# A list of moves behind a list scheduler: 97 operations change places on their engines

## Chip, cores and metric

The kernel runs on one core of a Trainium2 chip. The metric is the device time of one execution in microseconds (us), the median of three runs. A core has a matmul engine (TensorE, PE in the profile; its weight loads are PEld), VectorE (DVE), ScalarE (ACT), GpSimd (POOL), and SyncE (SP), which here only issues DMAs.

## What is computed

Three layers follow one another. Attention over 2 batches, 8 heads, 768 positions of 64 numbers, where each position sees the first 8 positions and its last 96:

```python
scores = scale * np.matmul(q, k.transpose(0, 1, 3, 2)) + bias       # bias: slope of the head times the distance
scores = np.where(is_global | is_local, scores, -1000000000.0)
a = np.exp(scores - max); a = a / (sum + 1e-09)
x = np.matmul(a, v)                                                 # heads put side by side: (2, 768, 512)
```

Then a layer that mixes each position with the one before it, and a normalised feed-forward layer:

```python
xk = mu_k * x + (1.0 - mu_k) * x_prev
xr = mu_r * x + (1.0 - mu_r) * x_prev
x = 1.0 / (1.0 + np.exp(-(xr @ w_r))) * (np.maximum(xk @ w_k, 0.0) ** 2 @ w_v)
xn = (x - mu) / np.sqrt(var + 1e-06) * g_ln
return x + np.maximum(xn @ w_ch1, 0.0) @ w_ch2                      # w_ch1: 512 x 2048
```

The weights arrive as words of 64 bits and are made into 32-bit numbers on the chip.

## The kernel before

**Stages.** The attention goes by 12 blocks of 128 positions. For each, queries and keys are loaded (`plan_loads`), turned by TensorE (`plan_turn`, L443), multiplied to scores (`plan_scores`, L496), given the bias and their minimum by VectorE (`least`, L509), exponentiated by ScalarE (`exp`, L515), turned (L546) and multiplied with the values (`values` in `plan_weighted`, L561). `plan_out` scales and turns the result: GpSimd adds a small constant to the sums (L587), VectorE takes the reciprocal (L588), GpSimd spreads it over a tile (L591), TensorE turns it (four instructions, L598), ScalarE copies it back, and VectorE multiplies. Every 256 positions are a group of the mixing layer (`plan_mix`, L699 to L711; its products L755 and L791). In the last layer both products are done by a scheme of seven half-size products with each operand split in a high and a low part (L1089, L1190 to L1192).

**Weights.** `plan_words` makes a piece of 128 x 512 weights: a DMA into a tile (L625), a copy of the high words with a factor by ScalarE (L343) or GpSimd (L347), and three integer steps of VectorE (L628, L629, L630). `split` then makes the high part (ScalarE, L636) and the low part (L640). The third and fourth piece of w_r have a tile of their own, `s1`; the others take turns in two tiles `stage`.

**Array forms.** Scores have operands of 64 rows (the code calls this "rows"), value products have 64 output columns ("columns"), and all others use the whole array. One value product of a block and four heads is 8 or 16 instructions in the trace, one score product 8.

**Order.** Every function registers operations with `Plan.op`: the engines that may do it with an estimated time, the cells read and written, the tiles, and a due time. There are 2222. `Plan.play` then builds the order: of the operations whose inputs are done and whose tiles are free it takes the one that can start first by its estimates, then the one due first, gives it to an engine and issues it. A change of form is counted with 95 ns (`SWITCH`). Each engine runs its instructions in the order of issue and waits for results of the others; PE, DVE, ACT and POOL keep the order written down. `first` (L911 on) registers the whole program and calls `play`.

Of the kernel before, what the change touches and what calls it, by code (L numbers as in the profile page):

```python
# [43 lines left out]
UP, LEAD = 15.6, 10.0  # L44
WARM = 9
FILL = {0: 4, 1: 3, 2: 3, 3: 2}
SCALE = 0.125
BIG = 2.0**38
SM_EPS = 1e-9
# [3 lines left out]
def slope(h):  # L53
    return 2.0 ** (-8.0 * (h + 1) / H)
# [56 lines left out]
class Plan:  # L111
# [29 lines left out]
        self.ops.append((engines, fn, deps, rooms, due, size, mode))  # L141
        return i

    def play(self):
        n = len(self.ops)
        wait = [len(x[2]) for x in self.ops]
        users = [[] for _ in self.ops]
        for i, x in enumerate(self.ops):
            for d in x[2]:
                users[d].append(i)  # L150
        ready = [0.0] * n
        by = {}
        free = {}
        live = {}
        open_ = [i for i in range(n) if not wait[i]]
        dma, mode = 0.0, ""
        trace = []
        while open_:
            best = None
            for i in open_:  # L160
                engines, _, _, rooms, due, _, _ = self.ops[i]
                at = ready[i]
                ok = True
                for x in rooms:
                    if x.tile is None:
                        if live.get(x.tag, 0) < x.bufs:
                            f = free.setdefault(x.tag, [0.0] * x.bufs)
                            at = max(at, f[0])
                        else:
                            ok = False  # L170
                if not ok:
                    continue
                for e, ns in engines.items():
                    t = max(at, self.clock[e])
                    if len(engines) > 1 and any(max(at, self.clock[g]) + m < t + ns for g, m in engines.items() if g != e):
                        continue
                    key = (t, due, i, e)
                    if best is None or key < best:
                        best = key
            if best is None:  # L180
                raise RuntimeError("no operation can go: " + str([(i, [x.tag for x in self.ops[i][3] if x.tile is None]) for i in open_][:20]))
            t, _, i, e = best
            engines, fn, _, rooms, _, size, way = self.ops[i]
            for x in rooms:
                if x.tile is None:
                    live[x.tag] = live.get(x.tag, 0) + 1
                    free[x.tag].pop(0)
                    x.tile = x.make()
            self.now = t
            fn(e)  # L190
            end = t + engines[e]
            if e == "PE" and way != mode:
                end += self.SWITCH
                mode = way
            self.clock[e] = end - self.OVERLAP.get(e, 0.0)
            if size:
                dma = max(dma, end) + size / 190.0
                end = dma + 1900.0
            trace.append((t, end, e, i))
            for x in rooms:  # L200
                x.left -= 1
                x.end = max(x.end, end)
                if not x.left and not x.hold:
                    live[x.tag] -= 1
                    free[x.tag].append(x.end + self.LAG)
                    free[x.tag].sort()
            open_.remove(i)
            for u in users[i]:
                ready[u] = max(ready[u], end + self.LAG)
                wait[u] -= 1  # L210
                if not wait[u]:
                    open_.append(u)
        assert not any(wait), [i for i in range(n) if wait[i]][:20]
        return trace


class Fast:
# [80 lines left out]
    def query_scale(self):  # L298
        self.qs = self.t([P, 4, 1], "qs")
        for h in range(H):  # L300
            self.nc.gpsimd.memset(self.qs[(h % 2) * D : (h % 2 + 1) * D, h // 2, :], -SCALE / slope(h))

# [172 lines left out]
    def plan_scores(self, i):  # L475
# [25 lines left out]
        op = p.op({"PE": 3.4 * w}, scores, reads, [("S", i)], banks + [self.Q, self.K], due, mode="rows")  # L501
        for x in range(FILL.get(i, 0)):
            self.filler(op, due + 2)
# [407 lines left out]
    def first(self, last):  # L911
# [13 lines left out]
        with self.tc.manual_schedule(engines=ORDERED):  # L925
# [7 lines left out]
            rooms = [self.token("rt", 2), self.token("rt", 2), self.token("e", 2)]  # L933
# [23 lines left out]
            end = self.due(24) + 8  # L957
# [15 lines left out]
            self.plan_second(at[NG])  # L973
            p.op({"DVE": 3000}, lambda e: last(), due=at[NG] + 150, behind=[self.step[8]["P1"]])
            p.op({"PE": 20}, lambda e: self.tc.mark_branch_hint_location("skip", "LikelyTaken", engines=[*ORDERED, mybir.EngineType.SP]), behind=[self.step[8]["P1"]], due=-6.0)
            self.trace = p.play()

    def plan_second(self, start):

# [252 lines left out]
def general_attention(tc, a, w, x_dram, ident):  # L1232

    nc = tc.nc
    with tc.tile_pool(name="ga1", bufs=1) as c1, tc.tile_pool(name="ga2", bufs=2) as c2, \
# [19 lines left out]
        for b in range(B):  # L1255
            for h in range(H):
                t = {}
                for x in "qkv":
                    t[x] = c2.tile([P, NB, D], F32, tag=x, name=x)
                    nc.gpsimd.dma_start(t[x], a[x][b, h].rearrange("(n p) d -> p n d", p=P))  # L1260
                for x, s in (("q", SCALE), ("k", 1.0)):
                    t[x + "T"] = c2.tile([D, S], F32, tag=x + "T", name=x + "T")
# [174 lines left out]
```

## Time and profile before

| what | before |
|---|---|
| median of 3 runs | 535.83 us (535.5 to 535.83) |
| the profiled execution's own time | 535.59 us |
| its span, first to last instruction | 533.8 us |
| TensorE busy | 524.3 us, 3231 matmuls |
| VectorE busy | 411.5 us |
| ScalarE busy | 302.7 us |
| GpSimd busy | 274.7 us |
| DMA | 40.52 MB, 76 GB/s in the mean |

Attention and mixing overlap up to some 130 us; from there to 268 us the mixing layer's last products run, and the seven-product scheme from 268 us to the end. An instruction's row in a timeline has its start, its length and in brackets the idle time of its engine before it with what ended that. Neighbouring instructions of one kind are one row with a count (x16). Lengths of matmul rows include the pipeline, so a time per instruction is taken from one row's start to the next row's start.

### The profile page before, as it was taken

What the parts mean: (1) busy time and instruction counts of PE and PEld (TensorE: products, weight loads), DVE (VectorE), ACT (ScalarE), POOL (GpSimd) and SP (SyncE); (2) the same over time, 40 slices, a digit from 0 to 9 for tenths busy, and PEclk for the clock granted to TensorE, in tenths of its full rate; (3) what the DMA queues carried; (4) which work ended last, traced back from release to release, by engine and by line L of the source; (5) the groups of instructions that cost most, each with busy time, mean ns of one, the idle gap of its engine ahead of it and who ended that gap; (6) DMA issues with size and microseconds to landing.
All of it is one profiled execution on the core that took longest, in us unless ns stands there. A gap on an engine that the chain in (4) does not pass through costs nothing.

```text
span 533.8 us, 8958 instructions
## 1 busy us (share of the span) xinstructions
PE 524.3 (98%) x3231; PEld 457.1 (86%) x3231; DVE 411.5 (77%) x817; ACT 302.7 (57%) x660; POOL 274.7 (51%) x346
## 2 busy tenths in 40 slices
PE   8999999999999999999999999999999999999997
PEld 6877787879899888889887898889998898989885
DVE  5899988965997437559889687778799878878564
ACT  3899998886454135474667454654555545365320
POOL 2487866846753121242238463773865758487300
PEclk9999999999999999999999999999999999999999
DMA  7996474301220000022022003122130312311024
GB/s 160 247 230 184 135 198 121 96 24 26 93 80 2 0 2 1 0 80 80 0 80 79 1 6 115 39 80 80 41 118 1 118 41 61 98 41 39 1 79 160
DMA packets 52110, 40.52 MB, mean 76 GB/s; under 512 B 40928, under 2 KB 41184, under 8 KB 52064
## 3 DMA queue, kind: packets, MB, share of 16 engines
q1 hardware_dynamic: 51200, 39.01, 25.9%
q10 hardware_dynamic: 864, 0.92, 0.5%
q8 instruction: 26, 0.43, 0.3%
q14 instruction: 20, 0.16, 0.1%
HBM read 36.77 MB, written 3.15 MB: 75 GB/s over the span
## 4 chain that ended last, share of the span: by engine, by line
PE 86%; DVE 5%; ACT 4%; POOL 2%; issue 1%; DMA 1%; SPq 0%; ACTq 0%; DVEq 0%
PE b L1089 20%; PE b L791 13%; PE b L1190 8%; PE b L1192 8%; PE b L1191 8%; PE b L755 5%; PE b L828 4%; PE b L830 4%; PE b L829 4%; PE b L561 3%; PE b L496 3%; PE b L546 3%; PE b L443 1%; PE b L527 1%; ACT t0l L515 1%
## 5 line engine op out<-in xcount | busy, mean ns | idle before, releaser
L630 DVE SCALAR_TENSOR_TENSOR cv<-cv,stage 128x512 int32<-128x512 int32 x50 | 45.2, 906 | 2.1 <-DVE stage L629 0.5
L515 ACT ACTIVATE t0l<-t0l,mn 128x232 f32<-128x232 f32 (+1 forms) x96 | 44.3, 467 | 4.3 <-DVE mn L509 4.3
L629 DVE SCALAR_TENSOR_TENSOR stage<-stage 128x512 int32<-128x512 int32 x50 | 46.0, 919 | 0.7
L699 POOL TENSOR_SCALAR rt<-xg,vec 128x256 f32<-128x256 f32 x48 | 31.4, 667 | 19.7 <-DVE m L806 8.6
L1206 DVE TENSOR_TENSOR xg<-b,xg 128x512 f32<-128x512 f32 (+1 forms) x51 | 34.3, 674 | 8.0 <-PE b L1192 6.7
L1108 POOL TENSOR_TENSOR h<-rt,h 128x384 fp32r<-128x384 f32 x28 | 33.4, 1194 | 8.3 <-ACT h L343 8.1
L1108 POOL TENSOR_TENSOR h<-e,h 128x384 fp32r<-128x384 f32 x14 | 15.4, 1103 | 42.7 <-ACT h L343 42.6
L1104 ACT ACTIVATE e<-e 128x384 f32<-128x384 f32 x16 | 8.4, 526 | 48.5 <-DVE e L1097 48.5
L628 DVE TENSOR_SCALAR stage<-stage 128x512 int32<-128x512 int32 x50 | 35.1, 702 | 0.5 <-DMA stage<-in_moe_w_ch_dram 0.5
L704 DVE SCALAR_TENSOR_TENSOR rt<-xg,vec,rt 128x256 f32<-128x256 f32 x48 | 31.0, 691 | 2.4 <-POOL rt L699 2.4
L509 DVE CUSTOM_DVE_ANT_0 t0l<-b,ln 128x232 f32<-128x232 f32 x80 | 27.6, 391 | 5.9 <-PE b L496 5.9
L791 PE MATMUL b<-b0l,t1l 128*128 128x256 f32 x144 | 31.9, 282 | 0.0
L1196 DVE TENSOR_TENSOR xg<-b,xg 128x1024 f32<-128x1024 f32 x23 | 28.0, 1218 | 4.9 <-PE b L1192 4.6
L866 POOL TENSOR_SCALAR st<-st 128x1 f32<-128x1 f32 x12 | 3.8, 315 | 52.4 <-DVE st L863 46.5
L546 PE MATMUL b<-ident,t0l 128*128 128x128 f32 x176 | 28.5, 281 | 0.0
L343 ACT ACTIVATE cv<-stage 128x512 f32<-128x512 f32 x41 | 27.2, 664 | 1.4 <-POOL s L640 0.9
L1089 PE MATMUL b<-t0h,s 128*128 128x384 f32 x128 | 28.0, 340 | 0.0
L1033 ACT ACTIVATE cv<-cv,vec 128x256 f32<-128x256 f32 x32 | 14.6, 502 | 23.5 <-DVE cv L630 23.4
L1089 PE MATMUL b<-t1h,s 128*128 128x384 f32 x128 | 27.6, 337 | 0.0
L640 POOL TENSOR_TENSOR s<-cv,s 128x384 fp32r<-128x384 f32 (+1 forms) x22 | 24.9, 1135 | 4.9 <-ACT s L636 4.9
L755 PE MATMUL b<-s,h 128*128 128x512 f32 x96 | 25.8, 405 | 0.0
L1089 PEld LDWEIGHTS b<-t1h,s 128*128 128x128 f32 x128 | 23.2, 188 | 2.8
(315 smaller groups left out, 1706.0 us busy)
## 6 DMA issues: line engine op xcount, KB each, us to landing
stage<-in_moe_w_ch_dram SPq DMA_DIRECT2D x26, 512.0 KB, 3.9
stage<-in_moe_w_k_dram SPq DMA_DIRECT2D x8, 512.0 KB, 4.5
stage<-in_moe_w_v_dram SPq DMA_DIRECT2D x8, 512.0 KB, 3.6
stage<-in_moe_w_ch_dram SPq DMA_DIRECT2D x12, 256.0 KB, 3.1
b0l<-in_q_dram SPq DMA_DIRECT2D x7, 256.0 KB, 4.5
h<-in_v_dram SPq DMA_DIRECT2D x6, 256.0 KB, 4.3
h<-in_v_dram SPq DMA_DIRECT2D x6, 192.0 KB, 3.1
stage<-in_moe_w_r_dram SPq DMA_DIRECT2D x2, 512.0 KB, 4.7
```

The source lines that it names most:

```text
L515: nc.scalar.activation(t, t, AF.Exp, bias=mn.tile[:, k : k + 1], scale=-1.0, accum_out=sm.tile[:, h : h + 1])
L546: nc.tensor.transpose(b.tile[:, c, k * P : (k + 1) * P], tp.tile[:, o : o + P], self.ident)
L628: p.op({"DVE": 500}, lambda e: nc.vector.tensor_scalar(low(), low(), 29, None, ALU.logical_shift_right), [R], [(R, 1)], [raw], due - 1.3, ...
L629: p.op({"DVE": 760}, lambda e: nc.vector.scalar_tensor_tensor(low(), high(), -(1 << 31), low(), ALU.bitwise_and, ALU.bitwise_or), [R, (R, ...
L630: p.op({"DVE": 760}, lambda e: nc.vector.scalar_tensor_tensor(y(), y(), 3, low(), ALU.logical_shift_left, ALU.bitwise_or), [(R, 2)], [C], ...
L755: nc.tensor.matmul(b.tile, *seq[s], start=s == 0, stop=s == 11)
L791: nc.tensor.matmul(o, l, r, start=s == 0, stop=s == 11)
L1089: nc.tensor.matmul(acc(x), lhs(i, c, n), rhs(r, j, c), start=y == 0, stop=y == 5)
L1108: lambda e: (nc.vector if e == "DVE" else nc.gpsimd).tensor_tensor(o(1), V(y), o(0).bitcast(F32), ALU.subtract),
L1190: nc.tensor.matmul(ps, hi, wh, start=f == 0, stop=False)
L1191: nc.tensor.matmul(ps, hi, wl, start=False, stop=False)
L1192: nc.tensor.matmul(ps, lo, wh, start=False, stop=f == 1)
```

## The change

`play` is cut in three. `choose` finds the order as before. `moved` takes 97 pairs (x, y) and puts operation x just before operation y on the engine that they share; then it merges the queues of the engines again, with the tiles' limits kept. `play` issues the result.

```diff
+MOVES = (
+    (507, 548), (715, 162), (149, 599), (690, 478), (597, 590), (204, 189), (250, 628), (288, 284),
...
-    def play(self):
+    def choose(self):
...
+    def moved(self, chosen):
...
+        for x, y in MOVES:
+            q = lists[home[x]]
+            q.remove(x)
+            q.insert(q.index(y), x)
+            rank[x] = rank[y] - 0.5
...
+            for e, q in lists.items():
+                if place[e] < len(q) and self.ops[q[place[e]]][2] <= done:
+                    i = q[place[e]]
+                    new = {x for x in self.ops[i][3] if x not in made}
+                    if all(live.get(x.tag, 0) + sum(z.tag == x.tag for z in new) <= x.bufs for x in new):
+                        heads.append((rank[i], e, i))
+            _, e, i = min(heads)
...
+    def play(self):
+        for e, i in self.moved(self.choose()):
+            _, fn, _, rooms, _, _, _ = self.ops[i]
+            for x in rooms:
+                if x.tile is None:
+                    x.tile = x.make()
+            fn(e)
```

The instructions are the same ones, and each stays on its engine. 91 different operations are named: 31 of VectorE, 27 of TensorE, 17 of GpSimd, 12 of SyncE, 10 of ScalarE. Counted over the whole queue of TensorE, two neighbouring operations differ in array form 88 times before and 78 times now: value products of one block come together in four places, and score and value products stand side by side in four more. Line numbers of the new file are 58 higher in the functions shown here (L561 is L619).

Four places follow. A row has the line, the operation, the tiles out<-in and the size; a tile's last number only counts tiles, and differs between the files.

SyncE at the start of the program, from the query load of block 2 (b0h<-in_q) on, before; u is the tile of keys, s1 that of the third and fourth piece of w_r:

```order
L402 DMA b0h_15_140<-in_q_dram 128x8x64
L353 DMA h1_1_74<-in_v_dram 96x8x64
L354 DMA h1_1_74<-in_v_dram 32x8x64
L625 DMA stage_16_144<-in_moe_w_r_dram 128x1024
L356 DMA b0h_15_140<-in_k_dram 128x8x64
L625 DMA s1_17_147<-in_moe_w_r_dram 128x1024
L356 DMA h1_1_74<-in_v_dram 128x8x64
L625 DMA s1_17_147<-in_moe_w_r_dram 128x1024
L353 DMA h1_1_74<-in_v_dram 96x8x64
L354 DMA h1_1_74<-in_v_dram 32x8x64
L353 DMA u_13_126<-in_k_dram 96x8x64
L354 DMA u_13_126<-in_k_dram 32x8x64
```

The same place now, from the second block's keys (the first two rows) on; the query load stands ahead of what is shown:

```order
L411 DMA u_13_126<-in_k_dram 96x8x64
L412 DMA u_13_126<-in_k_dram 32x8x64
L411 DMA u_13_126<-in_k_dram 96x8x64
L412 DMA u_13_126<-in_k_dram 32x8x64
L683 DMA s1_20_157<-in_moe_w_r_dram 128x1024
L411 DMA h1_1_74<-in_v_dram 96x8x64
L412 DMA h1_1_74<-in_v_dram 32x8x64
L683 DMA stage_21_161<-in_moe_w_r_dram 128x1024
L414 DMA b0h_15_136<-in_k_dram 128x8x64
L414 DMA h1_1_74<-in_v_dram 128x8x64
L683 DMA s1_20_157<-in_moe_w_r_dram 128x1024
```

The last two rows of before, the fourth block's keys, now stand third and fourth, ahead of both s1 loads.

GpSimd between 19 and 31 us of the profile, before; s1 is the raw tile, cv its copy, sm the softmax sums:

```order
L591 COPY xg_24_178<-sm_29_194 128x4x128
L640 TENSOR_TENSOR s0_39_233<-cv_38_232,s0_39_233 128x512
L425 COPY h1_1_74<-h1_1_74 32x512
L640 TENSOR_TENSOR s0_39_233<-cv_57_329,s0_39_233 128x512
L347 TENSOR_SCALAR cv_66_377<-s1_17_147 128x512
L587 TENSOR_SCALAR sm_53_304<-sm_53_304 128x8
L591 COPY xg_24_178<-sm_53_304 128x4x128
L640 TENSOR_TENSOR s0_39_233<-cv_66_377,s0_39_233 128x512
L347 TENSOR_SCALAR cv_77_437<-s1_17_147 128x512
L425 COPY h1_1_74<-h1_1_74 32x512
```

The same place now:

```order
L649 COPY xg_24_178<-sm_29_194 128x4x128
L698 TENSOR_TENSOR s0_38_231<-cv_37_230,s0_38_231 128x512
L483 COPY h1_1_74<-h1_1_74 32x512
L698 TENSOR_TENSOR s0_38_231<-cv_56_324,s0_38_231 128x512
L405 TENSOR_SCALAR cv_65_372<-s1_20_157 128x512
L405 TENSOR_SCALAR cv_66_374<-s1_20_157 128x512
L645 TENSOR_SCALAR sm_53_304<-sm_53_304 128x8
L649 COPY xg_24_178<-sm_53_304 128x4x128
L698 TENSOR_TENSOR s0_38_231<-cv_66_374,s0_38_231 128x512
L483 COPY h1_1_74<-h1_1_74 32x512
```

The copy from the fourth piece (before: cv_77, now cv_65) has gone from behind the low part L640 to the place ahead of the third piece's copy.

TensorE at 62 to 66 us, before; yy holds the turned exponentials, h1 the values, xg the spread reciprocals that L598 turns:

```order
L546 MATMUL b45_141_875<-ident_60,t0l_18_153 128x128 x6
L561 MATMUL b6_145_902<-yy_41_243,h1_1_74 64x128 x8
L598 MATMUL b3_147_916<-ident_60,xg_135_831 128x128 x4
L561 MATMUL b6_145_902<-yy_41_243,h1_1_74 64x128 x8
L546 MATMUL b45_151_942<-ident_60,t0l_18_153 128x128
L496 MATMUL b2_152_947<-b0h_15_140,b0l_12_123 128x128
```

The same place now:

```order
L604 MATMUL b45_141_875<-ident_60,t0l_16_142 128x128 x6
L656 MATMUL b3_146_906<-ident_60,xg_135_833 128x128 x4
L619 MATMUL b6_148_915<-yy_41_243,h1_1_74 64x128 x16
L604 MATMUL b45_151_942<-ident_60,t0l_16_142 128x128
L554 MATMUL b2_152_947<-b0h_15_136,b0l_12_123 128x128
```

The turns of xg now come first, and the value products of both halves of the block's heads follow in one piece (x16 calls, 32 instructions in the trace).

VectorE at 270 to 273 us, before; L640 makes low parts of weights, L878 subtracts for the normalised input:

```order
L640 TENSOR_TENSOR s1_408_3109<-stage_385_2903,s1_408_3109 128x512
L640 TENSOR_TENSOR s1_408_3109<-cv_398_3028,s1_408_3109 128x384
L640 TENSOR_TENSOR s1_408_3109<-stage_388_2925,s1_408_3109 128x512
L878 TENSOR_TENSOR h1_322_2349<-ln_403_3066,h1_322_2349 128x256 x2
L842 SCALAR_TENSOR_TENSOR xg_415_3160<-e_358_2671,b6_401_3049 128x512
```

The same place now:

```order
L698 TENSOR_TENSOR s1_408_3109<-stage_385_2903,s1_408_3109 128x512
L698 TENSOR_TENSOR s1_408_3109<-cv_398_3028,s1_408_3109 128x384
L936 TENSOR_TENSOR h1_322_2349<-ln_403_3066,h1_322_2349 128x256 x2
L698 TENSOR_TENSOR s1_408_3109<-stage_388_2925,s1_408_3109 128x512
L900 SCALAR_TENSOR_TENSOR xg_415_3160<-e_358_2671,b6_401_3049 128x512
```

The two subtractions L878 now stand ahead of the last of the three L640.

## Rows read from the trace of the kernel before

**Rows 1.** Page of the kernel before: busy time of each engine, granted clock by slice.
```profile
PE 524.3 (98%) x3231; PEld 457.1 (86%) x3231; DVE 411.5 (77%) x817; ACT 302.7 (57%) x660; POOL 274.7 (51%) x346
...
PEclk9999999999999999999999999999999999999999
```

**Rows 2.** Page: the chain that ended last, shares of the span by engine.
```profile
PE 86%; DVE 5%; ACT 4%; POOL 2%; issue 1%; DMA 1%; SPq 0%; ACTq 0%; DVEq 0%
```

**Rows 3.** Windows: us, then busy us (instructions) of each engine, clock, DMA share, GB/s.
```profile
66.00:130.00 64.00, 64.00 (x566) 53.09 (x562) 47.16 (x145) 53.55 (x147) 41.30 (x52) 1.00 0.35 92
...
300.00:500.00 200.00, 200.00 (x996) 179.99 (x995) 160.06 (x233) 103.04 (x203) 124.88 (x138) 1.00 0.19 59
```

**Rows 4.** Chain of waits, 7 to 70 us: start us, us, what the chain goes through.
```profile
26.88 0.39 ACT t0l L515
...
45.07 1.29 POOL h L711
...
57.78 0.72 DVE xg L345
...
62.76 0.80 POOL h L425
```

**Rows 5.** Timeline of TensorE, 42 to 47 and 111 to 120 us: start us, us, instruction.
```profile
44.25 1.97 PE L561 MATMUL b<-yy,h 128*64 128x128 f32 x32
46.15 0.44 PE L546 MATMUL b<-ident,t0l 128*128 128x128 f32 x2
...
116.89 0.60 PE L546 MATMUL b<-ident,t0l 128*128 128x128 f32 x4
117.32 0.60 PE L598 MATMUL b<-ident,xg 128*128 128x128 f32 x4
117.85 1.05 PE L496 MATMUL b<-b0h,b0l 64*128 64x232 f32 x8
```

**Rows 6.** Timeline of TensorE, 63 to 67 us (in brackets idle time, what ended it).
```profile
63.60 1.09 PE L561 MATMUL b<-yy,h 128*64 128x128 f32 x16 [0.57 <-POOL h L425]
64.62 0.66 PE L598 MATMUL b<-ident,xg 128*128 128x128 f32 x4
...
66.24 0.33 PE L546 MATMUL b<-ident,t0l 128*128 128x128 f32 x1
```

**Rows 7.** Timeline of GpSimd, 54 to 68 us.
```profile
58.67 0.80 POOL L591 COPY xg<-sm 128x512 f32<-128x512 f32 x1 [0.20 <-DVE b0h L345]
...
63.50 0.81 POOL L591 COPY xg<-sm 128x512 f32<-128x512 f32 x1
```

**Rows 8.** Timeline of GpSimd, 20 to 34 us.
```profile
23.76 0.86 POOL L347 TENSOR_SCALAR cv<-s 128x512 f32<-128x512 f32 x1
...
28.22 0.84 POOL L347 TENSOR_SCALAR cv<-s 128x512 f32<-128x512 f32 x1
```

**Rows 9.** Timeline of VectorE, 23 to 29 us.
```profile
25.28 0.69 DVE L630 SCALAR_TENSOR_TENSOR cv<-cv,s 128x512 int32<-128x512 int32 x1
...
26.44 0.40 DVE L509 CUSTOM_DVE_ANT_0 t0l<-b,ln 128x232 f32<-128x232 f32 x1 [0.17 <-PE b L496]
```

**Rows 10.** SyncE's timeline; DMAs of 7 to 27 us; loads of tile s, issue to landing.
```profile
14.74 2.65 SPq L625 DMA_DIRECT2D s<-in_moe_w_r_dram  x1
...
DMA packets 12383, 4.69 MB, mean 234 GB/s; under 512 B 11869, under 2 KB 11869, under 8 KB 12381
...
DMA to landing us min/median/max: 6.3/8.0/9.6
```

**Rows 11.** Timeline of VectorE, 266 to 276 us.
```profile
271.44 0.69 DVE L640 TENSOR_TENSOR s<-stage,s 128x512 fp32r<-128x512 f32 x1
272.04 0.88 DVE L878 TENSOR_TENSOR h<-ln,h 128x256 f32<-128x256 f32 x2
...
273.88 0.69 DVE L862 BATCH_NORM_STATS2 st<-xg 128x6 f32<-128x512 f32 x1 [0.36 <-ACT ln L876]
```

**Rows 12.** Timeline of TensorE, 262 to 297 us.
```profile
273.90 0.66 PE L871 MATMUL b<-ident,ln 128*128 128x128 f32 x4 [0.65 <-ACT ln L876]
```

More of the change, by code (lines that the diff above doesn't have):

```diff
@@ L46 @@
 FILL = {0: 4, 1: 3, 2: 3, 3: 2}
+MOVES = (
[13 rows of a table added]
+)
 SCALE = 0.125
@@ L142, in op @@
         return i
-    def play(self):
+    def choose(self):
         n = len(self.ops)
+        left = {x: x.left for o in self.ops for x in o[3]}
+        made = set()
         wait = [len(x[2]) for x in self.ops]
@@ L164, in play @@
                 for x in rooms:
-                    if x.tile is None:
+                    if x not in made:
                         if live.get(x.tag, 0) < x.bufs:
@@ L180, in play @@
             if best is None:
-                raise RuntimeError("no operation can go: " + str([(i, [x.tag for x in self.ops[i][3] if x.tile is None]) for i in open_][:20]))
+                raise RuntimeError("no operation can go: " + str([(i, [x.tag for x in self.ops[i][3] if x not in made]) for i in open_][:20]))
             t, _, i, e = best
-            engines, fn, _, rooms, _, size, way = self.ops[i]
+            engines, _, _, rooms, _, size, way = self.ops[i]
             for x in rooms:
-                if x.tile is None:
+                if x not in made:
                     live[x.tag] = live.get(x.tag, 0) + 1
                     free[x.tag].pop(0)
-                    x.tile = x.make()
-            self.now = t
-            fn(e)
+                    made.add(x)
             end = t + engines[e]
@@ L198, in play @@
                 end = dma + 1900.0
-            trace.append((t, end, e, i))
+            trace.append((e, i))
             for x in rooms:
-                x.left -= 1
+                left[x] -= 1
                 x.end = max(x.end, end)
-                if not x.left and not x.hold:
+                if not left[x] and not x.hold:
                     live[x.tag] -= 1
@@ L214, in play @@
         return trace
+    def moved(self, chosen):
+        rank, home, lists = {}, {}, {}
+        for k, (e, i) in enumerate(chosen):
+            rank[i], home[i] = float(k), e
+            lists.setdefault(e, []).append(i)
+        for x, y in MOVES:
[3 more added lines that the diff above has]
+            rank[x] = rank[y] - 0.5
+        left = {x: x.left for o in self.ops for x in o[3]}
+        place, done, made, live, order = dict.fromkeys(lists, 0), set(), set(), {}, []
+        while len(order) < len(chosen):
+            heads = []
+            for e, q in lists.items():
[5 more added lines that the diff above has]
+            _, e, i = min(heads)
+            place[e] += 1
+            done.add(i)
+            order.append((e, i))
+            for x in self.ops[i][3]:
+                if x not in made:
+                    made.add(x)
+                    live[x.tag] = live.get(x.tag, 0) + 1
+            for x in self.ops[i][3]:
+                left[x] -= 1
+                if not left[x] and not x.hold:
+                    live[x.tag] -= 1
+        return order
+    def play(self):
[5 more added lines that the diff above has]
+            fn(e)
 class Fast:
@@ L975, in first @@
             p.op({"PE": 20}, lambda e: self.tc.mark_branch_hint_location("skip", "LikelyTaken", engines=[*ORDERED, mybir.EngineType.SP]), behind=[self.step[8]["P1"]], due=-6.0)
-            self.trace = p.play()
+            p.play()
     def plan_second(self, start):
```

12 rows, old and new, of the table MOVES are left out of this document.

## The prediction

> **What bounds the kernel now.** I read the share of each engine first [rows 1]: TensorE is busy for 98% of the span and its granted clock is at full speed in every slice, so the clock plays no part. The chain that ended last says the same with an exception [rows 2]: TensorE has 86% of it, the other engines some 11%. Then the stretches [rows 3]: from 66 to 130 us and from 300 to 500 us TensorE has no idle time, so what is taken from its queue there comes off the end, and what other engines do there doesn't count while it stays early enough. In between, two places are set by other engines. The first is 26.5 to 63.6 us [rows 4]: the chain goes through ScalarE's exponentials (26.88), GpSimd (45.07), VectorE (57.78) and GpSimd again (62.76) before TensorE has it back at 63.60. TensorE looks busy there, with short waits, but a delay at the start of the stretch is handed on from one to the next and comes out at its end. The second is 268 to 295 us, where VectorE leads.
>
> My sums are made against the profiled execution, 535.59 us, of which 533.8 are the span and 1.8 lie around it. The median of the three runs is 0.24 higher; a change of 0.2%, about what a measurement of this kernel can tell from none, is 1.07 us. So "same" here means 534.76 to 536.90.
>
> **1. Fewer changes of array form.** No instruction goes or comes; TensorE changes form 78 times in place of 88. Price, from starts to starts: 32 value products in one piece last 1.90 us to the next start (44.25 to 46.15), 16 of them 1.02 (63.60 to 64.62) [rows 5, 6]. Two blocks of 16 apart cost 2.04, so a merge gives 0.14. In addition four turns last 0.53 when another form follows them (117.32 to 117.85) and 0.43 when none does (116.89 to 117.32) [rows 5]: 0.10 for one entry into a form. A merged pair thus saves 0.24, and a score block that comes to stand directly beside a value block saves 0.10. The new order has four merges (the products of the token blocks at 58.5, 63.6, 82.9 and 112.6 us) and four new neighbours (at 24, 70, 89 and 95 us); the merges at 82.9 and 112.6 each lose one neighbourhood they had, so they are worth 0.14. The total is 2 x 0.24 + 2 x 0.14 + 4 x 0.10 = 1.16 us. Only what lies in the TensorE-bound stretch counts: 3 x 0.10 + 2 x 0.14 = **-0.58 us**. The neighbour at 24 us and the merge at 58.5 lie under waits for other engines and are worth nothing; 63.6 is the next point.
>
> **2. The merge at 63.6 us.** Before, the first 16 products started as soon as GpSimd's copy of the value rows was done (63.60, after 0.57 of waiting), then came the four turns that need GpSimd's next copy (63.50 to 64.31 [rows 7]), done when TensorE came to them at 64.62 [rows 6]. Now the turns stand first. They can't start before 64.36 (GpSimd's end plus 0.05), last 0.53, and the 32 products another 1.90: the next instruction starts at 66.79, where it did at 66.24. That is +0.55. VectorE's copy of one column (0.72 of the chain at 57.78 [rows 4]) has been moved out of the way, but GpSimd's step behind it, at 58.67, had only 0.20 of idle time before it [rows 7], so at most 0.20 of that arrives: +0.35 at least. I take **+0.45 us**. So this form change is avoided at a loss: the saved 0.24 is already in the figure.
>
> **3. Loads and GpSimd's queue at 24 us.** This is the term that decides. SyncE's queue now has the load of the fourth token block's keys (128 x 512 numbers, 256 KB in two pieces) nine places earlier, ahead of the third and fourth weight pieces of w_r. And GpSimd's queue now has the copy from the fourth piece (before: 28.22) directly ahead of the copy from the third (before: 23.76) [rows 8]. GpSimd takes its instructions in order, so the third piece's copy, and behind it the copy of the softmax sums, waits until the fourth piece has landed. Behind that stands VectorE: its last step of the third piece (25.28) needs GpSimd's copy, and the instruction that ScalarE's chain starts from (26.44) stands two places behind it [rows 9]. Let L be the time when the fourth piece lands. GpSimd needs 0.84 + 0.86 for both copies, VectorE starts 0.05 later; its step moves from 25.28 to L + 1.75, and of this 0.17 was idle time before 26.44. The delay of the chain is L - 23.70, and not below 0.1, since GpSimd is free at 23.80.
>
> When does it land? Before, it was issued at 14.74 and took the longer of the two times shown, 9.6 us: 24.35 [rows 10]. The keys' 256 KB now go ahead of it; at the mean 234 GB/s of this stretch [rows 10] that is 1.1 us, so up to 25.4 (estimates from these rows). Against this: the third piece took only 6.3 us, so that the 9.6 may be one late straggler; without it the fourth could be there at about 23.5. So the bounds are +0.1 and +1.75. I take L = 24.7, nearer to the upper end since its row is the direct one: **+1.0 us**. In the same queue the query load of block 2 goes four places forward, and a weight, a key and two value loads come later by the same 1.1 us; what waits for those has most of that time, or is delayed side by side with GpSimd and not on top of it, so I add nothing.
>
> The Trainium skill (DMA: Bandwidth & Descriptors, Queues, rings and completion order) says that an engine's DMAs lie on one ring on each of the same 16 DMA engines, and that descriptors are taken in ring order. That speaks against the change: the fourth weight piece could not overtake the keys. By this rule alone L would be at the upper end, and the sum 0.75 higher; no row of the kernel before shows the reversed order.
>
> **4. 268 to 276 us.** VectorE's two subtractions (272.04) stand now ahead of one 0.60 us step (271.44) [rows 11]. So ScalarE's normalisation and GpSimd's subtractions, which wait for them, come 0.60 earlier. TensorE's wait of 0.65 at 273.90 goes [rows 12], but it isn't on the chain. VectorE's two idle times there (0.36 at 273.88 [rows 11], and as much again 1.7 us later) can close. The gain is between 0 and 0.6, as later waits of the same chain (up to 295) may take it back: **-0.3 us**.
>
> **5. The rest.** The other moves lie mostly in the stretches where TensorE has no idle time (66 to 268 us, and from 296 us on; [rows 3] show two of them), and most are of other engines. They are worth nothing as long as each result is still early enough; I put 0, with up to +0.3 if one is late. At the end of the program the order is the same.
>
> The sum is -0.58 + 0.45 + 1.0 - 0.3 + 0 = +0.57: 535.59 + 0.57 = 536.16, **536.2 us**.
>
> **Rivals.**
> *Faster.* The fourth piece lands before 23.8, so term 3 is 0.1; the earlier column copy gives its 0.20 and term 4 its full 0.6. Then -0.58 + 0.35 + 0.1 - 0.6 = -0.73 (534.86), which is still the same. It is faster if, in addition, GpSimd comes to the copy behind the turns at 63.6 us earlier, because its steps from 45 us on don't lie as tightly as the chain makes it look; then the merge there is worth its -0.24 in place of +0.35: -0.58 - 0.24 + 0.1 - 0.6 = -1.32, 534.3. For it: TensorE's idle time is small everywhere, and 1.16 us of work are gone. Against it: the chain from 26.5 to 63.6 runs through engines from which no work was taken.
>
> *Slower.* GpSimd stands at the head of its queue waiting for the fourth piece, at the full 1.75, and VectorE's idle times at 273 us don't close: -0.58 + 0.55 + 1.75 + 0 = +1.72, 537.3. It decides from L = 25.4 on with the other terms as taken (0.74 more than 24.7 brings the sum to 536.90). For it: the bytes put ahead, and that all that stands behind GpSimd's wait is on the chain. Against it: the straggler.
>
> *No effect.* Should the changes of form be hidden by TensorE's weight loads running ahead, term 1 is 0 and the sum is +0.45 + 1.0 - 0.3 = +1.15: 536.7. Against it stand the 0.53 and 0.43 of [rows 5].
>
> **How the numbers follow.** Same (terms near the taken ones, and the case without effect): 0.46. Slower, mainly by L: 0.28. Faster: 0.26. The point is that of the sum, 536.2. The range goes from 534.1 (the faster case's 534.3 and 0.2, about the spread of the runs, below) to 537.4 (the slower case's 537.3). The likeliest case's own range, with L from 24.0 to 25.4, is 535.5 to 536.9.
>
> **What would show it.** In the trace of after: TensorE's value products come in pieces of 32 at about 65 and 83 us, and one score or value block costs 0.10 less beside another. GpSimd sits idle before the copy at about 24 us, with the DMA of w_r as what ended it; VectorE's step at 25.3 and ScalarE's exponential at 26.9 come later by L - 23.7; TensorE has the chain back at 66.8 plus that delay, and the difference to before shrinks by 0.6 up to 130 us and stays until 268. The wait at 273.90 is gone. It is wrong if the fourth piece lands early, if the stretch to 63 us has slack that takes up the delay, or if TensorE shows new waits after 296 us.

## The result and the profile after

| | before | after |
|---|---|---|
| median | 535.86 us (8 runs beside it) | 538.77 us (8 runs, 537.67 to 541.79) |
| the profiled execution | 535.59 us, span 533.8 us | 538.95 us, span 537.2 us |
| TensorE, VectorE busy | 524.3, 411.5 us [rows 1] | 524.5, 407.5 us |

The changed kernel is slower: 2.9 us in the median, a ratio of 1.0051 to the kernel before, with a 95% interval of [1.0036, 1.0067]; ratios and intervals below are given in the same way. The 538.77 us lie above the range (537.4), so the prediction was wrong. The page of after, the busy line and the chain that ended last:

```profile
PE 524.5 (98%) x3231; PEld 458.4 (85%) x3231; DVE 407.5 (76%) x817; ACT 301.8 (56%) x660; POOL 273.7 (51%) x346
...
PE 88%; ACT 4%; DVE 3%; DMA 2%; POOL 1%; SPq 1%; issue 0%; DVEq 0%; ACTq 0%
```

TensorE has no more work than before, and VectorE 4 us less. Against [rows 2] DMA's share of the chain has doubled to 2%. Windows of after (us, then busy us and instructions of PE, PEld, DVE, ACT and POOL, clock, DMA share, GB/s):

```profile
20.00:45.00 25.00, 22.13 (x200) 17.20 (x199) 21.69 (x66) 20.64 (x59) 15.92 (x21) 1.00 0.86 194
...
66.00:130.00 64.00, 63.05 (x561) 52.50 (x562) 50.49 (x155) 53.88 (x149) 39.74 (x51) 1.00 0.38 100
...
300.00:500.00 200.00, 200.00 (x997) 180.05 (x996) 155.90 (x233) 101.17 (x201) 125.19 (x137) 1.00 0.19 59
```

The same first window of before:

```profile
20.00:45.00 25.00, 24.39 (x226) 19.02 (x226) 23.46 (x76) 22.82 (x64) 15.90 (x23) 1.00 0.83 197
```

TensorE is 2.3 us less busy between 20 and 45 us, with 26 instructions fewer; in the stretch from 66 to 130 us, where [rows 3] had no idle time, there is now nearly 1 us.

**Where it is lost.** I took the start of the same TensorE operation in both traces. The difference after minus before, the "shift" from here on, is at these times of before:

| at, us | 20.5 | 21.5 | 27.1 | 61.5 | 66.2 | 85.9 | 94.3 | 127 | 268 | 274 | 295 | 529 |
|---|---|---|---|---|---|---|---|---|---|---|---|---|
| shift, us | -0.16 | +2.11 | +2.74 | +2.59 | +3.26 | +3.76 | +3.63 | +3.40 | +3.32 | +2.46 | +3.33 | +3.61 |

Most of it comes in one step at 21 us. TensorE's waits of after, five of the longest (who waits for whom: us in total, times, longest):

```profile
PE b L501 <- ACT xg L401: 2.2, 1, 2.2
...
PE b L656 <- POOL xg L649: 0.9, 1, 0.9
PE b L929 <- ACT ln L934: 0.8, 1, 0.8
PE b L501 <- DMA u<-in_k_dram: 0.8, 1, 0.8
PE b L1248 <- DVE xg L1254: 0.8, 1, 0.8
```

The first is the step. It leads back through ScalarE to a load. Timelines of after, first SyncE's (start, length of the issue), then VectorE's, ScalarE's and TensorE's rows at 22 us:

```profile
13.13 0.45 SPq L683 DMA_DIRECT2D s<-in_moe_w_r_dram  x1
...
14.68 0.45 SPq L683 DMA_DIRECT2D stage<-in_moe_w_r_dram  x1
```

```profile
22.37 0.43 DVE L686 TENSOR_SCALAR stage<-stage 128x512 int32<-128x512 int32 x1 [3.12 <-DMA stage<-in_moe_w_r_dram]
...
22.37 0.69 ACT L401 ACTIVATE cv<-stage 128x512 f32<-128x512 f32 x1 [2.69 <-DMA stage<-in_moe_w_r_dram]
...
23.60 0.66 PE L501 MATMUL b<-ident,b0h 128*128 128x128 f32 x4 [2.21 <-ACT xg L401]
```

And the same load and VectorE step in the kernel before:

```profile
12.53 0.45 SPq L625 DMA_DIRECT2D stage<-in_moe_w_r_dram  x1
...
18.89 0.42 DVE L628 TENSOR_SCALAR stage<-stage 128x512 int32<-128x512 int32 x1
```

This load from issue to landing, in before and then in after:

```profile
DMA to landing us min/median/max: 4.9/4.9/4.9
```

```profile
DMA to landing us min/median/max: 7.7/7.7/7.7
```

This is the *second* piece of w_r. The prediction has it only as "a weight" that comes 1.1 us later and for which it adds nothing. In the kernel before it was issued at 12.53 and had landed at 17.4, 1.5 us before VectorE came to it. Now the fourth block's keys (256 KB) and the third piece (512 KB) are issued ahead of it; it goes out 2.15 us later and takes 7.7 us in place of 4.9, so it lands at 22.35. VectorE and ScalarE stand still for it, and TensorE behind ScalarE.

The Trainium skill (DMA: Bandwidth & Descriptors, Queues, rings and completion order) says that SyncE's DMAs lie on one ring on each of the same 16 DMA engines and that descriptors are taken in ring order, though a later one may finish its write before an earlier one. The trace agrees with the order as far as it goes: with 768 KB put ahead, the load landed 5 us later.

**What didn't happen.** GpSimd's copies, on which the prediction rested its third term, show no wait for the fourth piece. The timeline of GpSimd in after, which answers [rows 8]:

```profile
25.07 1.27 POOL L698 TENSOR_TENSOR s<-cv,s 128x512 fp32r<-128x512 f32 x1 [5.28 <-ACT s L694]
26.32 1.91 POOL L405 TENSOR_SCALAR cv<-s 128x512 f32<-128x512 f32 x2
```

GpSimd had stood 5.28 us before that for the second piece's high part; by 26.32 both pieces were there.

### The profile page after: what moved, and what is told of

Same layout as the page of the kernel before. It is cut to its first block, busy times and chain, and to the rows that moved or that the text cites. A ratio compares the mean times of both kernels' runs of the same rounds, so it can differ in the third digit from the quotient of the medians.

```text
span 537.2 us, 8949 instructions
## 1 busy us (share of the span) xinstructions
PE 524.5 (98%) x3231; PEld 458.4 (85%) x3231; DVE 407.5 (76%) x817; ACT 301.8 (56%) x660; POOL 273.7 (51%) x346
## 4 chain that ended last, share of the span: by engine, by line
PE 88%; ACT 4%; DVE 3%; DMA 2%; POOL 1%; SPq 1%; issue 0%; DVEq 0%; ACTq 0%
PE b L1147 21%; PE b L849 13%; PE b L1248 8%; PE b L1250 8%; PE b L1249 8%; PE b L813 5%; PE b L886 4%; PE b L888 4%; PE b L887 4%; PE b L554 3%; PE b L604 3%; PE b L619 3%; PE b L501 2%; DMA stage<-in_moe_w_r_dram 1%; ACT t0l L573 1%; DMA u<-in_k_dram 1%
## 5 line engine op out<-in xcount | busy, mean ns | idle before, releaser
L687 DVE SCALAR_TENSOR_TENSOR stage<-stage 128x512 int32<-128x512 int32 x50 | 44.5, 890 | 0.7
L688 DVE SCALAR_TENSOR_TENSOR cv<-cv,stage 128x512 int32<-128x512 int32 x50 | 42.8, 857 | 1.4
L757 POOL TENSOR_SCALAR rt<-xg,vec 128x256 f32<-128x256 f32 x48 | 32.6, 690 | 19.4 <-DVE m L864 8.6
L762 DVE SCALAR_TENSOR_TENSOR rt<-xg,vec,rt 128x256 f32<-128x256 f32 x48 | 34.5, 763 | 2.7 <-POOL rt L757 2.7
L401 ACT ACTIVATE yy<-b 128x1024 f32<-128x1024 f32 (+1 forms) x24 | 22.8, 949 | 5.4 <-PE b L604 5.0
```

Of the source, the lines that this page charges most:

```text
L401: self.nc.scalar.activation(out, x, AF.Copy, scale=scale)
L687: p.op({"DVE": 760}, lambda e: nc.vector.scalar_tensor_tensor(low(), high(), -(1 << 31), low(), ALU.bitwise_and, ALU.bitwise_or), [R, (R, ...
L688: p.op({"DVE": 760}, lambda e: nc.vector.scalar_tensor_tensor(y(), y(), 3, low(), ALU.logical_shift_left, ALU.bitwise_or), [(R, 2)], [C], ...
```

## Experiments

Each kernel is the changed one with entries of `MOVES` left out or added, or the kernel before with a few entries alone. Entries of one place: loads (120,3) query, (589,72) third piece, (167,589) keys; GpSimd's copies (597,590). The median of before beside the runs was 535.7 to 535.9 throughout.

### The loads, and GpSimd's copies

Three kernels take parts of the change away:

```diff
 e1  - (120, 3), (589, 72), (167, 589)
 e2  - (597, 590)
 e4  - (120, 3), (589, 72), (167, 589), (597, 590)
```

> The changed kernel with three of its 97 moves taken back, those of SyncE's loads at the start: the query load of block 2, the key load of block 3 and the third piece of w_r go back to their places. The other 94 moves stay. Theory A (the loads): in the changed kernel the second piece of w_r landed at 22.35 us and not at 17.43, VectorE and ScalarE stood idle for it for 3.12 and 2.69 us, and this alone is the +2.7 us that every later matmul shows; then the second piece is back at about 17.4, both idle times are gone, and what is left is the cost of GpSimd's order (0.1 to 0.7) and of the merges: 535.9 to 536.9 us. Theory B (the forecast's: GpSimd's copy of the fourth piece at the head of its queue): the copy order is still there, the loss stays: 538 us or more.

> The changed kernel with one move taken back: GpSimd copies from the third piece of w_r first again, and from the fourth behind it. Theory A (the loads): the second piece of w_r still lands at about 22.4 us, VectorE and ScalarE still wait about 3 us for it; GpSimd's order was worth 0.2 us at most: 538.5 to 538.8 us. Theory B (GpSimd's order): at least 1 us comes back, 537.7 us or less.

> The changed kernel without the three load moves and without GpSimd's exchanged copies; 93 moves stay, all changes of TensorE's form among them. Theory A: what is left are the saved changes of form (-0.58 us between 66 and 130 us), the waits that the merges at 63.6 and 82.9 us brought in the changed kernel (+0.67 and +0.48), and nothing lasting from 268 to 296 us: 535.9 to 536.6 us, no gain. A rival (C): with the delay at the start gone, the merges don't wait, and the time is about 0.6 us below before, 535.2 us.

Measured: e1 536.77 us, ratio 1.0021 [0.9999, 1.0042]; e2 538.71, 1.0053 [1.0031, 1.0076]; e4 536.21, 1.0008 [0.9985, 1.0031]. The three load moves cost 2.0 us in the medians (538.77 to 536.77; what this is made of follows below). GpSimd's exchange makes no difference that can be seen where the loads are moved as well (538.71, but e2's seven runs lie between 537.4 and 541.2); the trace of after, where its copies wait for nothing, says the same. In e1 VectorE's step on the second piece has no idle time before it again, and TensorE's shift at 21.5 us is -0.25:

```profile
19.08 0.42 DVE L685 TENSOR_SCALAR stage<-stage 128x512 int32<-128x512 int32 x1
```

The other way round, the kernel before with only the loads, and with only GpSimd's exchange:

```diff
 e3  + (120, 3), (589, 72), (167, 589)
 f5  + (597, 590)
```

> The kernel before with only the three moves of SyncE's loads. Theory A: the second piece of w_r lands at about 22 us, the two idle times of about 3 us are there, and the time is 2.5 to 3 us above before: 538.4 to 538.9 us. Theory B: without GpSimd's exchanged copies the loads do nothing, 535.9 us.

> The kernel before with one move: GpSimd copies from the fourth piece of w_r ahead of the third. The loads are in their old order, the fourth piece lands at 24.35 us. Theory B, by the forecast's formula: GpSimd waits for it, the chain at 26.4 us is 24.35 - 23.70 = 0.65 us later, and the time is 536.5 us. Rival: the stretch has slack for it, 535.9 us.

Measured: e3 537.66, 1.0031 [1.0022, 1.004], less than expected by some 0.7 us or more; f5 535.97, 0.9995 [0.9978, 1.0012]. In e3 VectorE waits for the second piece again, though for less time than in after. In f5 the mechanism of the predicted third term can be seen by itself, GpSimd's copies and then VectorE's next steps:

```profile
24.47 1.56 POOL L393 TENSOR_SCALAR cv<-s 128x512 f32<-128x512 f32 x2 [0.60 <-DMA s<-in_moe_w_r_dram]
...
26.06 0.69 DVE L676 SCALAR_TENSOR_TENSOR cv<-cv,s 128x512 int32<-128x512 int32 x1 [1.18 <-POOL cv L393]
26.97 0.35 DVE L555 CUSTOM_DVE_ANT_0 t0l<-b,ln 128x232 f32<-128x232 f32 x1
```

The fourth piece landed at 24.3. L - 23.70 gives 0.62; VectorE's step that [rows 9] show at 26.44 starts at 26.97, 0.53 later, and TensorE's shift is +0.48 at 34 us. So the formula was right for the start of the chain. But without the keys ahead the delay is worth about half a microsecond in the trace (0.40 to 0.50 from 34 to 268 us) and too little to be told from none in the median, and with the second piece late it is hidden.

### Which load

```diff
 f7 (of after)   - (597, 590)  + (582, 167), (121, 167)     second piece and block 2's keys ahead of the early keys
 f6a (of before) + (589, 72), (167, 589)                    without the query load
 f6b (of before) + (589, 72)                                third piece alone
 f4 (of before)  + (167, 589)                               keys alone, behind the second piece
```

> The changed kernel with the three load moves kept, but the second piece of w_r and the keys of block 2 put ahead of the fourth block's keys; GpSimd copies in the old order. Theory A in its narrow form (only the places of the second piece and of these keys count, not the early keys as such): the second piece lands before 18 us, VectorE and ScalarE don't wait for it, and the time is that of the changed kernel with the old loads and the old copies, 536.2 us. Rival: the early keys cost by themselves (bytes ahead of everything else, a longer issue on SyncE), 537.5 us or more.

> The kernel before with two of the three load moves: the fourth block's keys and the third piece of w_r go ahead; the query load of block 2 stays. Theory A: the 768 KB put ahead of the second piece of w_r are the cause, it lands at 21 to 22 us, and the time is 537.3 to 538 us, as with all three. Rival: the query load among the small loads, and the longer issue on SyncE that stands behind it (8.56 to 10.87 us), has a share; then 536.3 to 537 us.

> The kernel before with one move: the third piece of w_r ahead of the second, the early keys left where they were. Theory A (the second piece comes later by the bytes that are put ahead of it in SyncE's queue; 512 KB of the 768 KB that the three load moves put there, which cost 1.8 us together): two thirds of 1.8, +1.2 us, 537.0, VectorE waits for the second piece before its first integer step at about 20 to 21 us. Theory B (what costs are the early keys, the pieces' own order is nothing): 535.9, within 0.3 of before. If the whole +1.8 is there, the order of the pieces alone does it and the keys add nothing.

> The kernel before with one move: the fourth block's keys ahead of the third and fourth pieces of w_r, but behind the second. Theory A (only the second piece's delay costs): 535.9, within 0.3 of before, no idle time of VectorE for the second piece at 18.9 us; the third and fourth pieces land some 1.1 us later and nothing waits for the third. Theory B (the early keys cost by themselves, as the 0.95 us that stayed when the second piece was put ahead of them): +0.95, 536.8. By the prediction's own reading of the fourth piece (VectorE's copy of it stands behind): a shift only if GpSimd's copies at 24 to 28 us show a wait for s.

Measured: f7 537.16, 1.0021 [1.0004, 1.0039]: 1.55 of the 2.5 us between e2 and e4 come back, 0.95 stay, between the two expectations (these are differences of medians whose intervals are some 2 us wide). f6a 537.54, 1.0024 [1.001, 1.0038], 0.12 below e3: the query load has no share that the medians show. f6b 535.60, 0.9997 [0.9987, 1.0008]; f4 536.34, 1.0016 [0.9997, 1.0035]. The two moves together, f6a, cost +1.7; apart they cost -0.1 and +0.6. VectorE's step on the second piece in f6b, f6a and e3, in this order:

```profile
19.34 0.43 DVE L674 TENSOR_SCALAR stage<-stage 128x512 int32<-128x512 int32 x1 [0.32 <-DMA stage<-in_moe_w_r_dram]
```

```profile
19.94 0.43 DVE L674 TENSOR_SCALAR stage<-stage 128x512 int32<-128x512 int32 x1 [1.00 <-DMA stage<-in_moe_w_r_dram]
```

```profile
21.33 0.43 DVE L674 TENSOR_SCALAR stage<-stage 128x512 int32<-128x512 int32 x1 [0.98 <-DMA stage<-in_moe_w_r_dram]
```

Against 18.89 that is 0.45, 1.05 and 2.44 us later; TensorE's shift at 27 us was +0.05, +0.49 and +1.47. So the cost doesn't simply follow the bytes put ahead, as f6b's first theory had it (+1.2). The first half microsecond of the second piece's delay costs nothing: with 512 KB ahead it stays inside that, with 768 KB not. This explains why the third piece alone is free and the pair is not. (f6a's profiled execution, 536.53 us, is the fastest of its twelve, 1.0 below their median. In e3's TensorE was already 1.38 us late before that point, see the last section, so its row counts as a bound only.)

Neither expectation covered f4's +0.6. TensorE has no new wait in it; its shift is -0.11 at 66 us, and then it grows: +0.37 at 268, +0.43 at 300, +0.74 at 529. Between 300 and 530 us it goes in small steps at some two dozen places, most of them 8 to 28 ns later and a few 13 to 17 ns earlier. The same steps stand in all six kernels that had the early keys and in none of the nine that had not.

### Where two tiles lie

The steps led to the built programs. The tiles are placed in memory in the order in which `play` makes them. With the keys early, the tile of the exponentials, `t0l`, is made before the weight tile `s1`, and the two change places: s1 from byte 72768 of each partition to 85152, t0l from 89152 to 72768. No other tile of that memory moves. Three kernels tell the places from the transfers:

```diff
 def play(self):
...
+                if x.tile is None and x.tag == "s1" and not self.placed:     # g1; in g2 and g3 "t0l"
+                    self.placed = True
+                    z = next(z for op in self.ops for z in op[3] if z.tag == "t0l")     # "s1"
+                    if z.tile is None:
+                        z.tile = z.make()
                 if x.tile is None:
                     x.tile = x.make()
```

> The kernel before with its own order; only the two tiles s1 (weights) and t0l (exponentials) change places in memory, as they do when the early keys make t0l the one made first. Theory P (the keys' 0.6 us comes from where the two tiles lie): +0.6, 536.4 (535.74 + 0.6); in the trace TensorE falls behind by 0.3 us between 300 and 530 us in steps of 12 to 17 ns and nothing changes before 66 us. Theory K (it comes from the keys' transfer, and the places are nothing): 535.7, within 0.2 of before.

> The keys alone moved ahead of the third and fourth pieces, as in the run with that one move, but the tiles s1 and t0l lie where they lay before. Theory P: the 0.6 us are gone, 535.75, no steps between 300 and 530 us. Theory K: 536.35, as with the keys alone.

> The changed kernel, with all its 97 moves, but with the tiles s1 and t0l where they lay in the kernel before. Theory P: 0.3 to 0.7 us less than the changed kernel's 538.77, 538.1 to 538.5, TensorE's shift the same at 295 and 529 us. Theory K: 538.8. Both expect VectorE's wait for the second weight piece at 22 us to stay.

Measured: g1 536.45 us beside 535.80, g2 535.81, g3 538.14. The intervals are as wide as the effect (g1 1.0007 [0.999, 1.0023], g2 1.0006 [0.9984, 1.0029], g3 1.0037 [1.0024, 1.0051]), so the traces have to decide, and they do. g1 runs before's instructions in before's order; one and the same turn near 66 us and the last of TensorE's products, in before and then in g1:

```profile
66.24 0.33 PE L546 MATMUL b<-ident,t0l 128*128 128x128 f32 x1
...
529.56 0.28 PE L1192 MATMUL b<-w,h 128*128 128x256 f32 x1
```

```profile
66.21 0.33 PE L597 MATMUL b<-ident,t0l 128*128 128x128 f32 x1
...
530.24 0.28 PE L1243 MATMUL b<-w,h 128*128 128x256 f32 x1
```

It loses 0.68 us on the way, +0.29 by 268 and +0.38 by 300, at the same places and in the same steps as f4. With the places put back the steps are gone: in g2 the shift is 1.61 at 300 and 1.61 at 529 (1.49 of it from a late start), and in g3 3.10 and 3.05, where after had 3.34 and 3.61. So two tiles' places cost 0.6 to 0.7 us, and the early keys behind the second piece nothing. Of the 2.0 us of the three load moves some 0.6 are therefore places (538.77 to 538.14), and the rest goes with the late second piece. The places also cover most of the 0.95 that f7 left: behind 20.5 us its trace loses 1.09, that of e4 0.39.

Why the places matter wasn't tried. That s1 itself is read more slowly at 85152 would not cover it: of the 0.30 us that g1 loses between 300 and 530 us, by times from start to start, 0.17 come at products that read s1 and 0.13 at products that read neither tile, and between 160 and 268 us products that read neither lose 0.22 while those that read s1 gain 0.06. One thing that differs is that 72768 and 89152 are multiples of 64 and 85152 of 32 only.

### The merges and the form changes

```diff
 f3 (of before)  + (426, 427), (729, 730), (325, 357), (507, 522)
 f2 (of before)  + (280, 295), (371, 386)
```

> The kernel before with four moves of TensorE alone: three score blocks come to stand beside a value block (70, 89 and 95 us), and the value products of 112.6 and 118.8 us come together. By the forecast's prices 3 x 0.10 + 0.14 = 0.44 us less by 130 us in the trace, and 535.4 us. If a change of form costs nothing, 535.9 us and no shift in the trace.

> The kernel before with two moves: the value products of 63.6 us come together, and so do those of 82.9 us. If the merges bring waits of their own (the first for GpSimd's copy behind the turns, the second because a score block is pulled forward to where its banks of results are not yet free), the trace is about 0.4 us later at 66 us and another 0.5 at 86 us, and the time is 536.6 us. By the prices of the changes of form alone, 0.24 + 0.14 less: 535.4 us.

f3 does the four edits of TensorE's order that bring no wait by the prediction: 535.34 us, 0.9977 [0.9957, 0.9998]; the shift goes from -0.04 at 66 us to -0.64 at 127, and -0.55 stay. Priced at 0.44, measured 0.55: the three neighbours gave 0.14, 0.16 and 0.18 where each was priced at 0.10, the merge 0.13 for 0.14. So form changes cost about what [rows 5] show, or a little more, and the rival without effect falls.

f2 merges the products of the blocks at 63.6 and 82.9 us: 537.06, 1.0023 [1.0006, 1.004]; +0.65 at 66, +1.12 at 86, and it doesn't come back (+1.37 from 300 on). TensorE's timeline of f2:

```profile
64.40 0.66 PE L644 MATMUL b<-ident,xg 128*128 128x128 f32 x4 [1.33 <-POOL xg L637]
64.98 1.97 PE L607 MATMUL b<-yy,h 128*64 128x128 f32 x32
66.88 0.33 PE L592 MATMUL b<-ident,t0l 128*128 128x128 f32 x1
...
83.52 1.68 PE L542 MATMUL b<-b0h,b0l 64*128 64x232 f32 x8
85.14 1.97 PE L607 MATMUL b<-yy,h 128*64 128x128 f32 x32
```

The place at 83 us in before:

```profile
82.35 0.60 PE L598 MATMUL b<-ident,xg 128*128 128x128 f32 x4
82.88 1.09 PE L561 MATMUL b<-yy,h 128*64 128x128 f32 x16
83.91 1.05 PE L496 MATMUL b<-b0h,b0l 64*128 64x232 f32 x8
84.89 1.09 PE L561 MATMUL b<-yy,h 128*64 128x128 f32 x16
```

At 64 us the turns wait for GpSimd, as [rows 6, 7] let one expect. At 83 us the score block, which stood between the two halves, comes to stand ahead of them, 1 us earlier. It then takes 1.62 us to the next start in place of 0.98: no row says idle, but it is stretched by 0.64, while VectorE's minimum steps on scores run (L555, 83.39 to 84.66). That they still read the banks into which the block writes is the likely cause; it wasn't tried by itself.

### Leaving out what costs

f1 is the changed kernel without the loads, GpSimd's exchange, the two merges and two moves at 285 us; h1 leaves out six early moves more, and h2 six in the last layer:

```diff
 f1 (of after)  - (120,3), (589,72), (167,589), (597,590), (280,295), (371,386), (371,411), (371,411), (1285,1194), (1287,1280)
 h1 (of f1)     - (39,42), (92,94), (81,99), (108,109), (88,128), (715,162)
 h2 (of h1)     - (1190,1191), (1198,1213), (1341,1324), (1205,1301), (1292,1347), (1216,1357)
```

> The changed kernel without ten of its moves: the three load moves, GpSimd's exchanged copies, the merges of value products at 63.6 and 82.9 us (four entries), and in the last layer GpSimd's early low part of a weight piece and ScalarE's exchanged word copies. 87 moves stay, with 81 changes of form in place of 88. Theory A (loads cost 2 us, the two merges cost 0.4 to 0.7 each by waits they bring, GpSimd's early low part takes back what 268 us gained): all losses gone, the cheap form changes (-0.45) and part of the gain at 268 us (-0.3) stay: 534.7 to 535.4 us. Rival: the many other moves cost something as well, 535.8 us or more.

> The kernel without the ten moves that cost (534.5 us) less six more: four moves of TensorE before 27 us (three turns and one filler), one exponential of ScalarE, and GpSimd's first step of a mix at 37.8 us. In the trace of the former the matmuls were 0.24 us late at 27 us and 0.39 at 49 us, against 0 in the kernel before. If these six moves are the cause, 534.1 us; if not, 534.5 us.

> As the one before, less six moves of the last layer's start (VectorE, ScalarE and GpSimd between 280 and 300 us). In the trace of the kernel without the ten costly moves 0.8 us were won up to 274 us and 0.5 given back up to 295. If these six moves take it back, 0.5 less than the one before, 533.6 to 533.7 us; if the chain there takes it back anyway, no difference.

Measured: f1 534.51 us, 0.9972 [0.996, 0.9984]; h1 534.20, 0.9966 [0.9954, 0.9977]; h2 **533.80**, 0.9962 [0.9949, 0.9974], with 75 of the 97 moves. All three lie below both kernels; h2's median is 2.0 us under before and 5.0 under after. The steps between the three, 0.3 and 0.4, are no larger than the intervals. In f1 the shift is -0.09 at 66, -0.70 at 127, -0.88 at 268 and -1.29 at the end; windows of f1, which answer [rows 3]:

```profile
66.00:130.00 64.00, 64.00 (x567) 53.63 (x564) 47.95 (x146) 53.76 (x148) 40.62 (x52) 1.00 0.35 92
```

No idle time, and one matmul more in the same 64 us. What h1's and h2's six moves do by themselves stays open; as to h2, its profiled execution began with TensorE's slow start (last section), and its trace doesn't show the gain of the median.

## Why the prediction was wrong, by its steps

**1, form changes: price about right, one place wrong.** f3's four edits gave 0.55 for 0.44; in after they gave 0.40. But the merge at 82.9 us, entered as -0.14, cost +0.47. The term asked at 63.6 us what the order would wait for, and not at 82.9, where TensorE had no idle time. Even so, an instruction pulled forward by 1 us can come too early for what it needs. After's timeline of the place shows the stretched score block as in f2:

```profile
85.64 0.60 PE L656 MATMUL b<-ident,xg 128*128 128x128 f32 x4
86.17 1.68 PE L554 MATMUL b<-b0h,b0l 64*128 64x232 f32 x8
87.78 1.97 PE L619 MATMUL b<-yy,h 128*64 128x128 f32 x32
```

**2, the merge at 63.6 us: right in its mechanism, too small.** Predicted +0.45, between 0.35 and 0.55; measured +0.67 in after and +0.65 in f2, with the wait at the turns that the term named:

```profile
66.54 0.66 PE L656 MATMUL b<-ident,xg 128*128 128x128 f32 x4 [0.92 <-POOL xg L649]
```

**3, the loads: the right place, the wrong load.** This is the step that failed. It followed the fourth piece to GpSimd, where the order had changed, and settled the others with "what waits for those has most of that time ... so I add nothing". It also counted 1.1 us for each of them, the keys' 256 KB. But the third piece had been moved ahead of the second as well, so the second had 768 KB put ahead, an estimated 3.4 us at the 234 GB/s of [rows 10], and only 1.5 us between its landing and its use. Both could be read from the order and the trace of before. Measured: a shift of +2.1 at 21.5 us and +2.7 at 27 us, in place of +1.0 for the term; in g3, with the same queue, +1.9 and +2.5. The doubt that kept the term low, that the fourth piece's 9.6 us were one straggler, didn't hold either: in the ten profiled executions with the old loads it landed between 23.8 and 25.2 us, and the 23.5 of the prediction follows from none of its rows.

**4, 268 to 276 us: right at its place, then taken back.** The subtractions came forward, the wait of [rows 12] is gone, and the shift fell by 0.86 up to 274 us, more than the 0.6 that the term allowed:

```profile
276.42 0.60 PE L929 MATMUL b<-ident,ln 128*128 128x128 f32 x4
```

By 295 us it had all come back (+0.87), through later waits of the same chain, as the term's lower bound of 0 allowed:

```profile
292.30 0.66 PE L929 MATMUL b<-ident,ln 128*128 128x128 f32 x4 [0.78 <-ACT ln L934]
...
298.62 0.50 PE L1248 MATMUL b<-b0h,h 128*128 128x512 f32 x1 [0.76 <-DVE xg L1254]
```

In f1, without two of the moves there, 0.36 of it was kept from 268 to 295 us (-0.88 to -1.24).

**5, the rest: not nothing.** It allowed up to 0.3 for a late result. TensorE has no idle time from 130 to 268 us nor from 300 to 500, so no result was late there; two tiles had changed places, for 0.3 us of shift between 295 and 529 us and 0.63 in the medians (538.77 to 538.14). The order of each engine's queue doesn't show that.

The terms as measured in the shift: the loads +2.6 (at 61.5 us), the first merge +0.67, the second +0.47, the other form changes -0.40 up to 120 us, 0 from there to 295, +0.28 behind: 3.6, the shift at 529 us. The rival "Slower" had the right sign and stretch; its mechanism, GpSimd at the head of its queue, was not the one that decided, so that its 537.3 came nearest is luck.

## To carry over

When a load is moved forward, the loads to look at are those it passes: list each with the bytes now ahead of it, and the time between its landing and its first use. A merge that spares a form change pays only if everything pulled forward or held back by it was waiting for nothing. And a move can also change the order in which tiles are made, and so where they lie: compare the places of the tiles in the two built programs, not the order alone.

## What the runs showed of the hardware

**Where two tiles lie costs TensorE time.** With `s1` and `t0l` moved and every engine's instructions and their order unchanged (g1), TensorE falls behind by 0.68 us in sum; between 300 and 530 us it does so in steps of mostly 8 to 28 ns, at the same places in every kernel in which the two tiles lie so. Which access is slower, and why, is not shown.

**A slow start of TensorE.** In five profiled executions (e2's and f7's, for a shorter time those of e3, g2 and h2) TensorE's granted clock is 0.50, its level of 1.2 GHz, for some microseconds from about 8 us on. They are 1.4 to 4.6 us late by 17 us. Windows of e2 and, below, of before:

```profile
8.00:17.00 9.00, 8.89 (x43) 7.62 (x44) 4.42 (x20) 3.00 (x12) 0.00 (x0) 0.50 0.86 200
```

```profile
8.00:17.00 9.00, 8.88 (x77) 7.25 (x78) 6.80 (x32) 5.99 (x21) 1.00 (x3) 1.00 0.95 222
```

43 matmuls in place of 77. In these five TensorE had stood idle 0.99 to 1.16 us for the first keys before its clock fell, in the other fourteen profiled executions 0.39 to 0.93 us (0.42 in before). The row of e2:

```profile
6.54 0.41 PE L500 MATMUL b<-ident,u 128*128 128x128 f32 x2 [1.15 <-DMA u<-in_k_dram]
```

**Landing times vary.** With the three loads moved and the same queue, the second piece landed at 21.1 us in e2 and g3, at 21.3 in e3 and at 22.4 in after; the profile of after is the latest of the four. In f6a, where the query load is not moved, it landed at 19.9; one trace doesn't tell whether that load or the execution made the difference.
